# Shifts, scaled V and the normalising product on GpSimd in a gated attention and Mish kernel

## The chip, the cores and the metric

The kernel runs on one core of a Trainium2 chip. The metric is device time in microseconds. A core has TensorE (PE, matrix products), ScalarE (ACT, exponentials and tables), VectorE (DVE) and GpSimd (POOL); SyncE (SP) issues the DMAs here. TensorE writes only to PSUM, eight banks of 128 x 512 fp32; the others exchange tiles through SBUF.

## The reference

```python
g = sigmoid((x * gate_w).sum(-1, keepdims=True))       # x: 1 x 2048 x 640, bf16
qkv = (x @ wqkv), split into q, k, v of 32 heads of 20
a = softmax(q @ k.T * 20 ** -0.5) @ v, heads put together, @ wo
h = x @ w1 + b1                                        # 640 -> 1536
b = (h * tanh(softplus(h))) @ w2                       # Mish, 1536 -> 640
out = g * a + (1 - g) * b
```

## The kernel before

**Groups.** Attention runs over 32 groups: eight fours of heads (p) times four chunks of 512 queries (qc); the first five fours go chunk by chunk, the last three run inside each chunk. In a group, 16 blocks of 128 keys (j) times four heads make 64 score banks, 2048 in all. A visit of TensorE to the scores (L1118) multiplies row tiles of 32, up to four at once, one for each head. The products with V (L1211) are quads: four heads side by side in column tiles of 32, added up in one PSUM bank, acc, over the whole group. Dense work (q, k, v, Mish's two layers, the output product; all through product, L530) also uses column tiles. TensorE changes tiling between a visit to the scores and anything else.

**Two ways to an exponential.** ACT takes two or three score banks at once (L1168) and writes E. In their stead DVE can take a *set*, the four heads of one key block: four powers (power_of, L436) turn score banks into bf16 bit patterns through an int16 product, and two *shifts* (L494) add 43 and 86 to the patterns of the whole 128 x 2048 tile. The three tiles T are multiplied by V and by two scaled copies of V (VD, made by scale, L387), and their sum is the exponential's part. So a set takes four banks from ACT, costs DVE four powers and two shifts, and costs TensorE three V quads for one. VD is there for the last ND key blocks alone.

**The end of a group.** normalise (L1225) transposes acc from PSUM (L1232, a), takes reciprocals (L1246, b), multiplies by them (L1253, c) and stores four pieces of o to DRAM through SP. load_o (L871) brings o back transposed for the output product.

**The order.** Nothing is scheduled while the kernel runs. A planner in the kernel, the loop from L1614, steps through modelled time with fixed costs for each engine (an exponential of two banks 904 ns, a power or shift 600, a quad of 512 columns 216, a change of tiling 100) and writes out each engine's instructions in the order that it finds. Every engine then works strictly in that order and waits where a tile is not ready. `rule` holds the planner's choices, and PLAN changes them by progress in groups: LEAD is the number of sets that may be drawn for a group, KEEP3 and Q3 say when three banks may go to ACT at once, HEAT and HROOM when an idle TensorE multiplies by zeros (L1472). DVE's jobs wait in `dve_q`, with a priority and a time from which they are overdue.

**Buffers.** Seven of the eight PSUM banks are shared by scores and dense products; acc has its own. NHOLD tiles T hold sets, the other NTS - NHOLD (U_slots) hold shifted copies. NST staging tiles (st) carry q and k to DRAM, two tiles (ot) carry output rows, and two tiles (od) hold the transposed o.

Of the kernel before, what the change touches and what calls it, by code (L numbers as in the profile page):

```python
# [9 lines left out]
P = 128  # L10
# [48 lines left out]
INF = 1.0e18  # L59
# [3 lines left out]
def kernel(  # L63
# [35 lines left out]
    LOG2E = 1.4426950408889634  # L99
    ND = 6  # L100
    NLAST = 3
# [18 lines left out]
    NWARM = 6  # L120
    NTS = 9
    NHOLD = 5
    MOPEN = 3
# [12 lines left out]
    RING = 18  # L136
    NST = 2

# [26 lines left out]
    PLAN = {  # L165
        0.0: {'AHEAD': 5000.0, 'BEHIND': 6000.0, 'D2': 0.5, 'DQ': 1, 'DQ3': 2, 'DQ4': 2, 'ETIGHT': 0, 'HEAT': 0.9, 'HROOM': 0.0, 'KEEP3': 3, 'LEAD': 6, 'LOW': 0.5, 'MARGIN': 60.0, 'MERGE': 0, 'NEAR': 9, 'NOPEN': 3, 'PVMAX': 4, 'Q3': 2, 'ROOM': 200.0, 'SWTH': 520.0, 'VF': 0, 'VMIN': 2, 'WAIT1': 2000.0, 'WAIT2': 6000.0, 'WAITU': 100000.0},
        1.0: {'DQ3': 1, 'HROOM': 100.0, 'LOW': 0.6, 'MARGIN': 0.0, 'SWTH': 600.0, 'WAIT2': 100000.0},
        2.0: {'DQ': 2, 'MARGIN': 30.0},
        3.0: {'AHEAD': 1000.0, 'ETIGHT': 1, 'NEAR': 7, 'VF': 2, 'VMIN': 1, 'WAITU': 0.0},
        4.0: {'DQ': 3, 'LOW': 0.44, 'SWTH': 520.0, 'VF': 0},  # L170
        5.0: {'DQ4': 1, 'KEEP3': 2, 'LOW': 0.56, 'VMIN': 3, 'WAIT1': 0.0},
        6.0: {'LEAD': 5, 'MERGE': 1, 'Q3': 3},
        7.0: {'DQ': 2, 'NOPEN': 2},
        8.0: {'BEHIND': 4000.0, 'DQ4': 2, 'MERGE': 0},
        9.0: {'BEHIND': 2000.0, 'D2': 1.0},
        10.0: {'BEHIND': 6000.0},
        11.0: {'BEHIND': 4000.0, 'VMIN': 2, 'WAITU': 100000.0},
        12.0: {'BEHIND': 6000.0, 'MARGIN': 100.0},
        13.0: {'DQ4': 1, 'NOPEN': 4, 'PVMAX': 3},
        14.0: {'HEAT': 0.8, 'LOW': 0.41, 'MARGIN': 60.0, 'MERGE': 1, 'ROOM': 100.0},  # L180
        16.0: {'DQ': 1, 'DQ3': 3, 'NEAR': 12, 'ROOM': 300.0},
        17.0: {'MERGE': 0, 'SWTH': 250.0, 'VF': 2, 'WAIT2': 6000.0},
        18.0: {'PVMAX': 4, 'Q3': 1, 'WAIT1': 2000.0},
        19.0: {'BEHIND': 3000.0, 'ROOM': 100.0, 'VMIN': 1},
        20.0: {'LOW': 0.53, 'ROOM': 200.0},
        21.0: {'PVMAX': 2, 'SWTH': 300.0, 'WAIT2': 30000.0},
        22.0: {'LEAD': 6, 'MARGIN': 100.0, 'SWTH': 250.0},
        23.0: {'AHEAD': 5000.0, 'BEHIND': 2000.0, 'PVMAX': 4, 'SWTH': 450.0, 'WAIT1': -2000.0},
        24.0: {'DQ3': 0, 'DQ4': 0, 'LEAD': 5, 'MARGIN': 0.0, 'NEAR': 7, 'Q3': 2},
        25.0: {'BEHIND': 4000.0, 'DQ4': 3, 'KEEP3': 3, 'LOW': 0.41, 'WAITU': -200000.0},  # L190
        26.0: {'ETIGHT': 0, 'HROOM': 0.0, 'KEEP3': 2},
        27.0: {'HROOM': -200.0, 'NEAR': 9, 'ROOM': 100.0},
        29.0: {'AHEAD': 1000.0, 'PVMAX': 3, 'SWTH': 520.0, 'WAIT1': 2000.0, 'WAIT2': 100000.0},
        30.0: {'BEHIND': 6000.0},
        31.0: {'KEEP3': 0, 'VMIN': 2},
    }
# [289 lines left out]
    def d_shifts(d, t):  # L486
        G, j = d["G"], d["j"]
        pv_items[G].append((t, j, (0, d["T"], d["slot"])))

        def shift(i, t):  # L490
            slot = t_slot(U_slots, t)
            slot.users = 4
            tile_ = work.tile([P, 4 * QC], BF16, tag=slot.tag, name="T")
            nc.vector.tensor_scalar(  # L494
                out=tile_[:, :].bitcast(I16), in0=d["T"][:, :].bitcast(I16),
                scalar1=float(SHIFT[i]), scalar2=None, op0=ALU.add,
            )
            d["T%d" % i] = (tile_, slot)
            d["slot"].users -= 1
            d["slot"].free_at = max(d["slot"].free_at, t + 700.0)  # L500

        def can(t):
            return (
                pv_G[0] >= G and vd_ready.get(groups[G][0], INF) <= t
                and t_slot(U_slots, t) is not None
            )

        for i in range(1, NSH + 1):
            dve(
                t, t, 600.0, (lambda t, i=i: shift(i, t)), prio=2, can=can,  # L510
                done=lambda t, i=i: pv_items[G].append((t, j, (i,) + d["T%d" % i])),
            )

# [90 lines left out]
    def dense_chain(kind, i, c, start, due):  # L604
# [19 lines left out]
        def evac():  # L624
# [65 lines left out]
    def v_chain(sts, w, c0, n, start, due, gate=False):  # L690
# [18 lines left out]
        def evac():  # L709
# [174 lines left out]
    def load_b(s):  # L884
        if s not in bl and s < NS and bl_slots and b_left[s // NU] == 0:
# [3 lines left out]
            nc.sync.dma_start(out=bl[s][:, :], in_=b_dram[s * P : (s + 1) * P, :])  # L889

    def wo_chain(s, half, start, due):
        c, u = divmod(s, NU)
# [20 lines left out]
        def evac():  # L913
            ps = box["ps"]

            def copy(t):
# [308 lines left out]
    def normalise(G, ready):  # L1225
# [26 lines left out]
        def c(t):  # L1252
            nc.vector.tensor_tensor(  # L1253
                out=T2[i][:, :].rearrange("p (b r) -> p b r", r=32)[:, :, 0:DH],
# [23 lines left out]
        def c_done(t):  # L1278
# [4 lines left out]
            for k in range(4):  # L1283
# [6 lines left out]
                )  # L1290
            if p == NQ - 1:
                load_o(qc, D, t)
            elif p == NQ - NSB - 1 and qc == LQ:
                load_o(qc, (NQ - NSB) * HF, t)

# [127 lines left out]
    def step_pe(t):  # L1423
# [40 lines left out]
        def heat(room):  # L1464
# [6 lines left out]
            for t_ in range(4):  # L1471
                nc.tensor.matmul(  # L1472
                    acc[32 * t_ : 32 * t_ + DH + 1, :],
                    lhsT=zero_w[:, 0 : DH + 1], rhs=xT[:, 0, 0:QC], start=False, stop=False,
                    tile_position=(0, 32 * t_), skip_group_check=True,
# [236 lines left out]
```

## Time and profile before

| | us |
|---|---|
| median of 3 runs | 736.36 (731.82, 736.36, 736.46) |
| the profiled execution's own time | 730.75 |
| its span, first to last instruction | 729.0 |
| first and last exponential start | 10.9, 719.2 |
| first and last shift start | 47.4, 718.0 |
| ACT busy / DVE busy / GpSimd busy | 708.2 / 680.9 / 5.2 |

Busy times count overlapping instructions once, so busy time divided by the count is the pace of a group, while the mean of one is its length. Ends of matmuls are modelled, so TensorE is best read from the starts. TensorE's granted clock is 1.00 in each stretch of 100 us. Each row of the groups gives line, engine, operation, tiles written and read, shapes, count, busy time, mean ns of one, then idle time before it and what ended that.

### The profile page before, as it was taken

How to read it: one execution, taken by the hardware profiler on the slowest of the kernel's cores; microseconds unless marked ns; L12 is line 12 of the kernel's file. 1: busy time of each engine (PE TensorE's matmuls, PEld its weight loads, DVE VectorE, ACT ScalarE, POOL GpSimd, SP SyncE). 2: the span in 40 equal slices, each digit the busy share in tenths (PEclk: the TensorE clock that was granted, in tenths of full speed). 3: DMA queues.
4: the chain of work that ended last, by engine and by line, in shares of the span. 5: the costliest groups of instructions: out<-in, count | busy, mean ns of one | idle time of the engine just before them, and what ended most of it. 6: DMA issues, size and time to landing. Idle time of an engine off the chain costs nothing.

```text
span 729.0 us, 24381 instructions
## 1 busy us (share of the span) xinstructions
PE 714.5 (98%) x10390; PEld 233.5 (32%) x10390; DVE 680.9 (93%) x1214; ACT 708.2 (97%) x742; POOL 5.2 (1%) x12
## 2 busy tenths in 40 slices
PE   7999999999999999999999999999999999999987
PEld 4433332222222333333333222222333333333323
DVE  4499999999999989999999999899989999999987
ACT  6899999999999999999999999999999999999995
POOL 2000000000000000000000000000000000000000
PEclk9999999999999999999999999999999999999999
DMA  9511121131411211012130223311104210413421
GB/s 246 177 24 34 36 59 36 30 81 40 86 32 40 49 45 24 12 15 41 43 92 26 44 41 87 81 54 25 30 22 74 56 38 25 65 43 61 75 75 55
DMA packets 125612, 40.46 MB, mean 56 GB/s; under 512 B 91136, under 2 KB 124944, under 8 KB 125504
## 3 DMA queue, kind: packets, MB, share of 16 engines
q1 hardware_dynamic: 123904, 38.38, 24.1%
q8 instruction: 81, 1.33, 0.8%
q10 hardware_dynamic: 1600, 0.53, 0.3%
q14 instruction: 27, 0.22, 0.1%
HBM read 23.61 MB, written 12.79 MB: 50 GB/s over the span
## 4 chain that ended last, share of the span: by engine, by line
PE 72%; ACT 16%; issue 5%; DVE 4%; DMA 2%; SPq 1%; DVEq 0%
PE Sp L1118 25%; PE Sp L530 24%; PE Sp L1211 22%; ACT E L1168 16%; DVE T L436 2%; DVE T L494 1%; DMA w_top<-in_A_wqkv_dram 1%; PE Sp L1472 1%; DMA kT<-k_dram 1%; DVE st L632 0%; DMA out_dram<-ot 0%; DVE ot L925 0%; PE Sp L1653 0%; PE Sp L1329 0%; DMA q_dram<-st 0%
## 5 line engine op out<-in xcount | busy, mean ns | idle before, releaser
L1168 ACT ACTIVATE E<-Sp 128x1024 bf16<-128x1024 f32 (+1 forms) x726 | 677.0, 1114 | 6.4 <-PE Sp L1118 5.9
L436 DVE TENSOR_SCALAR T<-Sp 128x512 int16<-128x512 f32 (+1 forms) x572 | 375.6, 685 | 14.5 <-PE Sp L1118 13.6
L1118 PE MATMUL Sp<-qT,kT 32*128 32x512 bf16 x2048 | 290.9, 384 | 5.3 <-ACT E L1168 1.9
L494 DVE TENSOR_SCALAR T<-T 128x2048 int16<-128x2048 int16 x288 | 192.2, 680 | 0.7
L1118 PEld LDWEIGHTS <-kT 32*128 32x128 bf16 x2048 | 76.4, 91 | 272.9 <-issue 269.2
L1211 PE MATMUL Sp<-E,VA 128*21 128x512 bf16 x1472 | 140.4, 382 | 0.0
L1211 PE MATMUL Sp<-T,VD 128*21 128x512 bf16 x1152 | 106.1, 382 | 0.0
L530 PE MATMUL Sp<-w_sb,big 128*32 128x320 bf16 x1536 | 77.8, 301 | 0.0
L530 PE MATMUL Sp<-xT,w1t 128*32 128x512 bf16 x960 | 76.1, 384 | 0.2 <-DVE T L436 0.2
L1211 PEld LDWEIGHTS <-VA 128*21 128x21 bf16 x2048 | 44.0, 90 | 64.2 <-issue 55.7
L1211 PE MATMUL Sp<-T,VA 128*21 128x512 bf16 x576 | 54.5, 382 | 0.0
L530 PE MATMUL Sp<-xT,ws 128*32 128x512 bf16 x720 | 53.9, 383 | 0.0
L530 PEld LDWEIGHTS <-big 128*32 128x32 bf16 x1536 | 33.7, 95 | 27.7 <-issue 20.0
L1211 PEld LDWEIGHTS <-VD 128*21 128x21 bf16 x1152 | 26.9, 90 | 30.7 <-issue 25.7
L778 DVE TENSOR_SCALAR big<-Sp,b1f 128x512 bf16<-128x512 f32 x48 | 35.6, 742 | 1.1 <-PE Sp L530 0.8
L530 PE MATMUL Sp<-wo_sb,od 128*32 128x320 bf16 (+1 forms) x608 | 32.7, 302 | 2.0 <-DVE ot L925 2.0
L530 PE MATMUL Sp<-wv,xT 128*32 128x81 bf16 (+2 forms) x960 | 33.9, 258 | 0.2 <-DVE st L632 0.2
L632 DVE CAST st<-Sp 128x512 bf16<-128x512 f32 x36 | 24.6, 683 | 5.0 <-PE Sp L530 3.5
L530 PEld LDWEIGHTS <-w1t 128*32 128x32 bf16 x960 | 18.1, 94 | 27.7 <-issue 24.6
L1232 DVE STREAM_TRANSPOSE T<-Sp 128x512 f32<-128x512 f32 x32 | 22.7, 708 | 0.9 <-PE Sp L1211 0.6
L713 DVE CAST VA<-Sp 128x80 bf16<-128x80 f32 (+2 forms) x48 | 16.2, 373 | 7.1 <-PE Sp L530 7.1
L530 PEld LDWEIGHTS <-xT 128*32 128x32 bf16 x960 | 18.0, 96 | 14.6 <-issue 12.3
(72 smaller groups left out, 196.0 us busy)
## 6 DMA issues: line engine op xcount, KB each, us to landing
w1t<-in_B_w_dram SPq DMA_DIRECT2D x24, 320.0 KB
q_dram<-st SPq DMA_DIRECT2D x20, 128.0 KB
b_dram<-bt SPq DMA_DIRECT2D x16, 160.0 KB
bl<-b_dram SPq DMA_DIRECT2D x16, 160.0 KB
out_dram<-ot SPq DMA_DIRECT2D x16, 160.0 KB
qT<-q_dram SPq DMA_DIRECT2D x124, 20.0 KB
o_dram<-T SPq DMA_DIRECT2D x120, 20.0 KB
kT<-k_dram SPq DMA_DIRECT2D x28, 80.0 KB
```

The costliest lines, as they stand in the source:

```text
L436: nc.vector.tensor_scalar(out=dst.bitcast(I16), in0=src, scalar1=inv_sqrt_dh * LOG2E * 128.0, scalar2=127.0 * 128.0 + BETA, op0=ALU.mult, ...
L494: nc.vector.tensor_scalar(out=tile_[:, :].bitcast(I16), in0=d["T"][:, :].bitcast(I16), scalar1=float(SHIFT[i]), scalar2=None, op0=ALU.add,)
L530: nc.tensor.matmul(out_[k : k + 32], lhsT=lhsT[:, k : k + 32], rhs=rhs, tile_position=(0, k), **kw)
L632: nc.vector.tensor_copy(out=res["st"][:, :], in_=ps[:, :])
L713: nc.vector.tensor_copy(out=VA[:, sts[i], h0 : h0 + nh, 0:DH], in_=ps[:, i, 0:n].rearrange("p (h d) -> p h d", d=DH),)
L778: nc.vector.tensor_scalar(out=big[:, slot.tag, (ft % 2) * QC : (ft % 2 + 1) * QC], in0=ps[:, :], scalar1=b1f[:, ft : ft + 1], scalar2=None ...
L1118: nc.tensor.matmul(ps_cols, lhsT=kT[p][32 * t_ : 32 * t_ + 32, j * P : (j + 1) * P], rhs=qT[G][32 * t_ : 32 * t_ + 32, :], tile_position=( ...
L1168: nc.scalar.activation(E[:, x : x + n, :], ps, ACT.Exp, scale=inv_sqrt_dh,)
L1211: nc.tensor.matmul(acc[32 * t_ : 32 * t_ + DH + 1, :], lhsT=lhsT, rhs=rhs, start=(pv_done[G] == 0), stop=(pv_done[G] == pv_total[G] - 1), ...
L1232: nc.vector.transpose(out=st["T1"][:, :, :].rearrange("p b r -> p (b r)"), in_=acc[:, :])
L1472: nc.tensor.matmul(acc[32 * t_ : 32 * t_ + DH + 1, :], lhsT=zero_w[:, 0 : DH + 1], rhs=xT[:, 0, 0:QC], start=False, stop=False, tile_posit ...
```

## The change

It moves three kinds of work from VectorE to GpSimd: the shifts (but for the last group, NDV = 1), the scaled copies of V, and the product with the reciprocals (but for the last group). The planner gets a fourth engine with a queue `pool_q`, worked by (group, time), with costs of its own: 1840 ns for a shift and 140 until others see it, 620 for a product. A shift may now also start one group ahead if at least UEARLY = 2 tiles are free.

Buffers: ND 8 for 6, NTS 11 for 9, NHOLD 6 for 5 (so five U tiles for four), three st and three ot tiles, each with a time from which the planner holds it free. The transposed o lies in the columns of xT of its chunk and is fetched in two parts. The dummy products read w2_sb in place of xT. PLAN is another table throughout.

```diff
-    ND = 6
+    ND = 8
-    NTS = 9
-    NHOLD = 5
+    NTS = 11
+    NHOLD = 6
-    NST = 2
+    NST = 3
+    PCOST = 1840.0
+    PTAIL = 140.0
+    UEARLY = 2
+    NDV = 1
+    NOT = 3
     PLAN = {
-        0.0: {..., 'KEEP3': 3, 'LEAD': 6, 'Q3': 2, ...},
-        5.0: {..., 'KEEP3': 2, ...},
-        6.0: {'LEAD': 5, 'MERGE': 1, 'Q3': 3},
-        18.0: {..., 'Q3': 1, ...},
-        22.0: {'LEAD': 6, ...},
-        24.0: {..., 'LEAD': 5, 'Q3': 2},
-        25.0: {..., 'KEEP3': 3, ...},
-        26.0: {..., 'KEEP3': 2},
-        31.0: {'KEEP3': 0, 'VMIN': 2},
+        0.0: {..., 'KEEP3': 3, 'LEAD': 6, 'Q3': 2, ...},
+        2.0: {..., 'KEEP3': 2, 'Q3': 1, ...},
+        3.0: {'KEEP3': 1, ...},
+        4.0: {..., 'Q3': 2},
+        5.0: {..., 'KEEP3': 3},
+        6.0: {'KEEP3': 1, 'Q3': 1, ...},
+        7.0: {..., 'LEAD': 5, ...},
+        8.0: {'KEEP3': 3, 'LEAD': 7},
+        9.0: {..., 'Q3': 3, ...},
+        10.0: {..., 'Q3': 1, ...},
+        12.0: {..., 'KEEP3': 2, 'LEAD': 8, ...},
+        17.0: {..., 'LEAD': 5, ...},
+        21.0: {'LEAD': 7, 'Q3': 2, ...},
+        22.0: {'LEAD': 6, ...},
+        27.0: {..., 'LEAD': 5, ...},
+        29.0: {'Q3': 1, ...},
+        31.0: {..., 'LEAD': 3, ...},
     }
@@ make_vd
-            nc.vector.tensor_scalar(
+            nc.gpsimd.tensor_scalar(
                 out=VD[p][:, :, i, :],
...
-            dve(t, t, 200.0, (lambda t, i=i: scale(i, t)), prio=1, done=done)
+            pool_q.append((
+                (-1, t), 70.0 + 0.86 * ND * 4 * (DH + 1), lambda t: True,
+                (lambda t, i=i: scale(i, t)), done,
+            ))
@@ d_shifts
-            nc.vector.tensor_scalar(
+            eng = nc.vector if G >= NG - NDV else nc.gpsimd
+            eng.tensor_scalar(
                 out=tile_[:, :].bitcast(I16), in0=d["T"][:, :].bitcast(I16),
                 scalar1=float(SHIFT[i]), scalar2=None, op0=ALU.add,
             )
...
+            pool_q.append((
+                (G, t), PCOST, can, (lambda t, i=i: shift(i, t)),
+                (lambda t, i=i: pv_items[G].append((t, j, (i,) + d["T%d" % i]))),
+            ))
@@ load_o
-        od[qc] = work.tile([P, KT, QC], BF16, tag=f"od{qc % 2}", name="od")
+        if qc not in od:
+            od[qc] = xT[:, :, qc * QC : (qc + 1) * QC]
@@ normalise
-            dve(t, t, 140.0, b, prio=pr, done=lambda t: dve(t, t, 420.0, c, prio=pr, done=c_done))
+            dve(t, t, 140.0, b, prio=pr, done=lambda t: pool_q.append(
+                ((G - 0.5, t), 620.0, lambda t: True, c, c_done)
+            ))
...
-            nc.vector.tensor_tensor(
+            nc.gpsimd.tensor_tensor(
                 out=T2[i][:, :].rearrange("p (b r) -> p b r", r=32)[:, :, 0:DH],
...
+    def step_pool(t):
+        for it in sorted(pool_q, key=lambda it: it[0]):
+            if it[0][1] <= t and it[2](t):
+                pool_q.remove(it)
+                it[3](t)
+                it[4](t + it[1] + PTAIL)
+                return it[1]
+        return None
```

More of the change, by code (lines that the diff above doesn't have):

```diff
@@ L136 @@
     RING = 18
-    NST = 2
+    NST = 3
[3 more added lines that the diff above has]
+    NDV = 1
+    TRD = -0.2
+    FKD = -0.1
+    NOT = 3
     rule = Rule()
@@ L165 @@
     PLAN = {
[L166 to L169, printed above, removed]
@@ L170 @@
-        4.0: {'DQ': 3, 'LOW': 0.44, 'SWTH': 520.0, 'VF': 0},
-        5.0: {'DQ4': 1, 'KEEP3': 2, 'LOW': 0.56, 'VMIN': 3, 'WAIT1': 0.0},
-        6.0: {'LEAD': 5, 'MERGE': 1, 'Q3': 3},
[L173 to L194, printed above, removed]
@@ L195 @@
-        31.0: {'KEEP3': 0, 'VMIN': 2},
+        0.0: {'AHEAD': 2000.0, 'BEHIND': 6000.0, 'D2': 0.5, 'DQ': 3, 'DQ3': 2, 'DQ4': 2, 'ETIGHT': 1, 'HEAT': 0.7, 'HROOM': 0.0, 'KEEP3': 3, 'LEAD': 6, 'LOW': 0.5, 'MARGIN': 60.0, 'MERGE': 0, 'NEAR': 99, 'NOPEN': 5, 'PVMAX': 4, 'Q3': 2, 'ROOM': 200.0, 'SWTH': 250.0, 'VF': 0, 'VMIN': 1, 'WAIT1': 0.0, 'WAIT2': 6000.0, 'WAITU': -200000.0},
+        1.0: {'HEAT': 0.8, 'ROOM': 100.0},
+        2.0: {'DQ3': 1, 'KEEP3': 2, 'Q3': 1, 'ROOM': 200.0, 'VF': 2},
+        3.0: {'KEEP3': 1, 'MARGIN': 0.0, 'ROOM': 100.0},
@@ new lines @@
+        4.0: {'DQ4': 1, 'HROOM': -200.0, 'PVMAX': 2, 'Q3': 2},
+        5.0: {'AHEAD': 3000.0, 'KEEP3': 3},
+        6.0: {'KEEP3': 1, 'NOPEN': 4, 'Q3': 1, 'VF': 0},
+        7.0: {'D2': 1.0, 'DQ4': 3, 'LEAD': 5, 'LOW': 0.38, 'NOPEN': 5},
+        8.0: {'KEEP3': 3, 'LEAD': 7},
+        9.0: {'PVMAX': 4, 'Q3': 3, 'WAITU': 0.0},
+        10.0: {'DQ': 1, 'Q3': 1, 'VF': 2, 'WAIT2': 3000.0},
+        11.0: {'NOPEN': 3},
+        12.0: {'HEAT': 0.9, 'KEEP3': 2, 'LEAD': 8, 'NEAR': 12, 'NOPEN': 4, 'SWTH': 300.0, 'VF': 0},
@@ new lines @@
+        13.0: {'ETIGHT': 0, 'HEAT': 0.7, 'PVMAX': 3, 'VF': 2, 'WAITU': -200000.0},
+        15.0: {'HROOM': 0.0},
+        16.0: {'PVMAX': 4, 'WAITU': 0.0},
+        17.0: {'DQ4': 1, 'LEAD': 5, 'NEAR': 7, 'NOPEN': 5, 'WAITU': 100000.0},
+        18.0: {'HROOM': -200.0, 'PVMAX': 3},
+        19.0: {'NEAR': 99},
+        20.0: {'PVMAX': 2},
+        21.0: {'LEAD': 7, 'LOW': 0.53, 'PVMAX': 3, 'Q3': 2},
+        22.0: {'LEAD': 6, 'LOW': 0.6, 'NEAR': 7, 'ROOM': 200.0, 'WAIT1': -2000.0, 'WAITU': 0.0},
@@ L196 @@
+        23.0: {'HEAT': 0.8, 'MERGE': 1, 'NEAR': 5},
+        24.0: {'HEAT': 0.9, 'PVMAX': 4},
+        25.0: {'DQ4': 3, 'HROOM': 0.0, 'MERGE': 0, 'NEAR': 9, 'ROOM': 100.0},
+        27.0: {'AHEAD': 5000.0, 'LEAD': 5, 'PVMAX': 3, 'WAIT1': 0.0},
+        28.0: {'DQ': 2, 'MARGIN': 30.0, 'NOPEN': 4, 'VF': 1},
+        29.0: {'Q3': 1, 'VF': 0},
+        31.0: {'AHEAD': 2000.0, 'HROOM': 100.0, 'LEAD': 3, 'MARGIN': 0.0},
+        32.0: {'LOW': 0.56, 'VMIN': 3},
     }
@@ L354 @@
     dve_q = []
+    pool_q = []
     act_q = deque()
     seq = [0]
-    free = {"PE": 0.0, "ACT": 0.0, "DVE": 0.0}
+    free = {"PE": 0.0, "ACT": 0.0, "DVE": 0.0, "POOL": 0.0}
     mode = [None]
@@ L360 @@
     s_left = [64] * NG
-    idle = {"PE": 0.0, "ACT": 0.0, "DVE": 0.0}
+    idle = {"PE": 0.0, "ACT": 0.0, "DVE": 0.0, "POOL": 0.0}
     def dve(t, ready, cost, fn, prio=1, done=None, can=None, born=INF):
@@ L499, in shift @@
             d["slot"].users -= 1
-            d["slot"].free_at = max(d["slot"].free_at, t + 700.0)
+            d["slot"].free_at = max(d["slot"].free_at, t + PCOST + 100.0)
         def can(t):
[L503 to L506, printed above, removed]
+            if vd_ready.get(groups[G][0], INF) > t:
+                return False
+            n = sum(1 for s_ in U_slots if s_.users == 0 and s_.free_at <= t)
+            return n > 0 and (pv_G[0] >= G or (pv_G[0] == G - 1 and n >= UEARLY))
         for i in range(1, NSH + 1):
[L509 to L512, printed above, removed]
+            if G >= NG - NDV:
+                dve(
+                    t, t, 600.0, (lambda t, i=i: shift(i, t)), prio=2, can=can,
+                    done=lambda t, i=i: pv_items[G].append((t, j, (i,) + d["T%d" % i])),
+                )
+                continue
+            pool_q.append((
+                (G, t), PCOST, can, (lambda t, i=i: shift(i, t)),
+                (lambda t, i=i: pv_items[G].append((t, j, (i,) + d["T%d" % i]))),
+            ))
     def mm_pieces(n, fn, each):
@@ L639, in done @@
                 stored[(kind, i, c)] = t + 2500.0
+                slot.free_at = t + 2800.0
             return [(600.0, copy)], done
@@ L644, in dense_chain @@
             start, due, mm_pieces(KT, piece, MM), evac,
-            lambda t: x_ok(c, t) and (kind, i) in strips and t >= (5000.0, 10000.0)[min(i, 1)],
+            lambda t: x_ok(c, t) and (kind, i) in strips and t >= (5000.0, 10000.0)[min(i, 1)]
+            and stages[0].free_at <= t + 500.0,
         )
@@ L734, in v_chain @@
         return Chain(
-            start, due, mm_pieces(KT * len(sts), piece, max(65.0, width / 2.4)), evac,
+            start, due, mm_pieces(KT * len(sts), piece, max(36.0, width / 2.4)), evac,
             lambda t: t >= (0.0 if gate else W_ARRIVE) and all(x_ready.get(st, INF) <= t for st in sts),
@@ L869, with load_o @@
     LQ = NQC - 1
-    def load_o(qc, upto, t):
-        od[qc] = work.tile([P, KT, QC], BF16, tag=f"od{qc % 2}", name="od")
-        for k in range(-(-upto // P)):
+    def load_o(qc, blocks):
+        if qc not in od:
+            od[qc] = xT[:, :, qc * QC : (qc + 1) * QC]
+        for k in blocks:
             nc.sync.dma_start(
@@ L878, in load_o @@
             )
-        o_ready[qc] = t + 8000.0
     bl_slots = ["bl0", "bl1", "wkp"]
@@ L889, in load_b @@
             nc.sync.dma_start(out=bl[s][:, :], in_=b_dram[s * P : (s + 1) * P, :])
+    ot_free = {}
+    begun = set()
     def wo_chain(s, half, start, due):
@@ L900, in piece @@
                 box["ps"] = bank_tile([P, HALF])
+                begun.add(s)
                 load_b(s)
@@ L922, in copy @@
                     if half == 0:
-                        ots[s] = work.tile([P, D], BF16, tag=f"ot{s % 2}", name="ot")
+                        ots[s] = work.tile([P, D], BF16, tag=f"ot{s % NOT}", name="ot")
                     o = ots[s][:, cols]
@@ L934, in done @@
                     nc.sync.dma_start(out=out2d[s * P : (s + 1) * P, :], in_=ots[s][:, :])
+                    ot_free[s % NOT] = t + 6000.0
             return [(430.0, copy)], done
@@ L941, in wo_chain @@
                 s in bl or (len(bl_slots) > 0 and b_left[c] == 0)
-            ),
+            ) and (s in begun if half else tail or ot_free.get(s % NOT, 0.0) <= t),
         )
@@ L950 @@
         for u in range(NU):
-            chains.append(transpose_chain(NU * c + u, -1.0, 0.25 * c - 0.2 + 0.01 * u))
-        chains.append(first_k_chain(c, -1.0, 0.25 * c - 0.1))
+            chains.append(transpose_chain(NU * c + u, -1.0, 0.25 * c + TRD + 0.01 * u))
+        chains.append(first_k_chain(c, -1.0, 0.25 * c + FKD))
     for a in range(0, NS, 4):
@@ L1290, in c_done @@
                 )
[L1291 to L1294, printed above, removed]
+            last_p = NQ - 1 - (NSB if qc == LQ else 0)
+            early = last_p * HF // P
+            if p == last_p - 1 and qc != LQ:
+                load_o(qc, range(early))
+            elif p == last_p:
+                load_o(qc, range(early, -(-(p + 1) * HF // P)))
+                o_ready[qc] = t + 9000.0
+                if qc == LQ - 1:
+                    load_o(LQ, range((NQ - NSB - 1) * HF // P))
         dve(0.0, ready, 640.0, a, prio=0, done=a_done)
@@ L1473, in heat @@
                     acc[32 * t_ : 32 * t_ + DH + 1, :],
-                    lhsT=zero_w[:, 0 : DH + 1], rhs=xT[:, 0, 0:QC], start=False, stop=False,
+                    lhsT=zero_w[:, 0 : DH + 1], rhs=w2_sb[:, 0, 0:QC], start=False, stop=False,
                     tile_position=(0, 32 * t_), skip_group_check=True,
@@ L1607, in step_dve @@
         return cost
-    steps = {"PE": step_pe, "ACT": step_act, "DVE": step_dve}
+    def step_pool(t):
[6 more added lines that the diff above has]
+        return None
+    steps = {"PE": step_pe, "ACT": step_act, "DVE": step_dve, "POOL": step_pool}
     t = 0.0
@@ L1613 @@
     plan = sorted(PLAN)
-    while pv_G[0] < NG or chains or chain[0] or dve_q or act_q:
+    while pv_G[0] < NG or chains or chain[0] or dve_q or act_q or pool_q:
         while plan and prog[0] >= plan[0]:
@@ L1627 @@
                 ev[1](t)
-        for eng in ("DVE", "ACT", "PE"):
+        for eng in ("POOL", "DVE", "ACT", "PE"):
             if free[eng] <= t:
```

## The prediction

> **What bounds the kernel now.** I read the engine totals first, then the groups kept apart by shape, then single starts in a busy stretch.
>
> ```profile
> PE 714.5 (98%) x10390; PEld 233.5 (32%) x10390; DVE 680.9 (93%) x1214; ACT 708.2 (97%) x742; POOL 5.2 (1%) x12
> ```
>
> ```profile
> L1168 ACT ACTIVATE E<-Sp 128x1024 bf16<-128x1024 f32 x704 | 651.2, 1103 | 6.4 <-PE Sp L1118 5.9 <-ACT E L1168 0.2
> L436 DVE TENSOR_SCALAR T<-Sp 128x512 int16<-128x512 f32 x568 | 370.8, 681 | 14.5 <-PE Sp L1118 13.6
> L1118 PE MATMUL Sp<-qT,kT 32*128 32x512 bf16 x2048 | 290.9, 384 | 5.3 <-ACT E L1168 1.9 <-ACT qT L1338 1.0 <-DVE st L632 0.7
> L494 DVE TENSOR_SCALAR T<-T 128x2048 int16<-128x2048 int16 x288 | 192.2, 680 | 0.7
> ...
> L1168 ACT ACTIVATE E<-Sp 128x1536 bf16<-128x1536 f32 x21 | 31.4, 1495 | 0.0
> ...
> L1472 PE MATMUL Sp<-xT,zero_w 128*21 128x512 bf16 x176 | 15.6, 383 | 0.0
> ...
> L1253 DVE TENSOR_TENSOR T<-T,rec 128x320 bf16<-128x320 f32 x31 | 14.9, 481 | 0.2
> ```
>
> Three engines are full at once and GpSimd is empty. Busy divided by count is the pace, since neighbours overlap: an exponential of two banks costs ACT 651.2/704 = 0.925 us, a power costs DVE (370.8 + 4.8 of four merged ones)/576 = 0.652, a shift 0.667. The 288 shifts are two for each of 144 sets; each set is four powers. So DVE takes 576 of the 2048 score banks, ACT 704 x 2 + 21 x 3 + 1 = 1472.
>
> A PE busy share is modelled, so I look at starts in TensorE's timeline:
>
> ```profile
> 306.79 0.39 PE L1118 MATMUL Sp<-qT,kT 32*128 32x512 bf16 x3
> 307.12 0.40 PE L1211 MATMUL Sp<-T,VD 128*21 128x512 bf16 x4
> 307.34 0.39 PE L1211 MATMUL Sp<-E,VA 128*21 128x512 bf16 x4
> 307.66 0.39 PE L1118 MATMUL Sp<-qT,kT 32*128 32x512 bf16 x3
> ```
>
> A V quad costs 307.34 - 307.12 = 0.22. The loop of one visit to the scores and two quads takes 0.87, so a visit costs 0.87 - 0.44 = 0.43, whether it makes two, three or four banks: about half of it is the change to the other tiling and back. Nearly every start from 100 to 700 us keeps this spacing, so TensorE is really full, and so is ACT (starts 0.903 apart at the median). The waits count the visits, and show how little waits for DMA:
>
> ```profile
> PEld L1118 <- issue: 269.2, 722, 1.0
> ...
> DVE ot L925 <- DMA out_dram<-ot: 2.1, 1, 2.1
> ...
> DVE st L632 <- DMA q_dram<-st: 1.4, 1, 1.4
> ```
>
> TensorE's sum: 722 visits x 0.43 = 310; V quads (1472 + 1152 + 576)/4 = 800 x 0.22 = 176; 44 dummy quads (L1472, 176/4) x 0.22 = 10. The other 233 of 729 are dense products, start and end, which the change leaves as they are.
>
> **What moves, and the size of it.** The planner may draw sets up to LEAD for a group. Weighting LEAD by the groups in which it holds gives 168 before, of which 144 were drawn (0.857), and 195 after. With the same share: 167 sets, 23 more.
>
> ACT: 92 banks fewer x 0.925/2 = -42.5 us, so ACT alone would allow 729 - 42.5 = 686.5.
>
> DVE: 668 powers x 0.652 = 436, and the other work, 680.9 - 375.6 - 192.2 - 14.9 (products L1253) - 3.9 (scaled V) = 94, plus some 6 shifts of the last group, 4: 534 us. It stops being near a bound (76% of 706).
>
> TensorE: 46 more V quads x 0.22 = +10.1. ACT's 92 banks are 46 visits fewer x 0.43 = -19.8. Three-bank exponentials save half a visit each. Nine of the 21 in the trace lie at 430 to 475 us, in the stretch with Q3 = 1 (groups 18 to 23); the new rules hold Q3 at 1 for about 19 groups and a less loaded DVE gives banks back sooner. At 9 for six groups, 13 more groups are 20 more; KEEP3 = 1 in four groups takes me to 40, between 0 and 80: -20 visits, -8.6. Half the dummy quads go, between none and all (0 to -9.7): -4.8. Sum -23.1: 705.9, with ends 729 + 10.1 - 19.8 = 719.3 and 729 + 10.1 - 19.8 - 17.2 - 9.7 = 692.4.
>
> GpSimd shows no shift before. The nearest rows are its fills and its select:
>
> ```profile
> L328 POOL MEMSET VA<- 128x512 bf16 x1 | 2.4, 2367 | 0.0
> ...
> L1343 POOL MEMSET wo<- 128x640 bf16 x2 | 1.2, 631 | 5.0 <-PE Sp L1329 5.0
> masks.py:199 POOL TENSOR_SCALAR_AFFINE_SELECT ident<-ident 128x128 bf16<-128x128 bf16 x1 | 0.3, 292 | 0.1
> masks.py:197 POOL MEMSET ident<- 128x128 bf16 x1 | 0.2, 204 | 0.0
> L314 POOL MEMSET zero_w<- 128x32 bf16 x1 | 0.1, 124 | 0.3 <-POOLq L1696 0.3
> ```
>
> The dense fills lie on a line: (631 - 124)/608 = 0.834 ns an element, 97 ns fixed. For 2048 elements that is 1.81 us. A shift also reads; the select reads and takes 88 ns more than a fill of its size. If that is fixed, a shift takes 1.89; if it is per element (0.69 ns), 3.21. The strided fill of VA at 2367/512 = 4.6 ns an element (9.5 us) is far, as shifts are dense. DVE's 0.68 is the end below. I take 1.85, between the first two, since DVE's rows show reading beside writing: its fill of 128x1024 takes 0.91 us and its shift, which also reads, 0.68 for 4 KB a partition alike. The planner reckons with PCOST = 1.84, so its order fits if that is right. The product (320 elements, two inputs) lies between 0.36 and 0.81; 0.62 taken, near the middle. The scaled V (672 elements): 0.66 to 1.12; 0.70 taken. GpSimd's sum: 334 - 6 = 328 shifts x 1.85 = 607, 31 x 0.62 = 19, 16 x 0.70 = 11: 637 us. It can start where the first shift starts now, 47 us, and must end about 10 us before the last row: 694. That is inside 706, with 12 us of room.
>
> What the moves queue: TensorE's order is fixed at build time, so a V quad of a shifted tile that GpSimd has not finished holds every later matmul, and with it ACT. Until now DVE gave the tile after 0.67 us, now it comes 1.2 us later; UEARLY lets shifts start one group ahead and there are five U tiles for four, so I cost this at nothing; uncovered at each of 31 group changes it is 31 x 1.2 = 37 us. The products on GpSimd can stand behind one shift (1.85), and four stores of o each stand in SP's queue behind them, with later q and k loads behind those. These are needed a group (some 21 us) later: nothing, else 1.85 x 31 = 57. The third st and ot tiles end waits of 1.4 and 2.1 us on DVE, which is no longer the bound: 0 taken of -3.5 to 0. The transposed loads of o into xT are as many as before (19), most a group earlier; xT of a chunk is last read by dense products well before: 0, at worst one wait like the 3.89 us that a kT load shows in the chain.
>
> The Trainium skill speaks against such a move: GPSIMD Engine Reference, section "Elementwise — side-by-side cycle accounting", puts its best ordinary loop at 1.8 cycles an element, which as an estimate would be 3.07 us a shift, though the same section lets a body of one or two operations run at 1.03 cycles, 1.76 us. By the first the sum would be some 1100 us, by the second the forecast stands.
>
> **Rivals.** (1) GpSimd becomes the bound, the case on the slow side. Its price is 57 us of start and end, 30 of products and scaled V, and 328 x p for the shifts, so it decides from p = (729 - 87)/328 = 1.96 us, only 6% over what I take. At 2.1 the span is 776; at 3.21, reading paid per element, 1140. For it: the narrow margin and that no row shows GpSimd at such a form. Against: dense fills of four sizes (1, 32, 128 and 640) lie on the one line. Chance 0.2. The skill's 1.8 cycles is this rival.
>
> (2) DVE and GpSimd block each other in SBUF. The one strided fill beside DVE fills took 2367; the next dense fill took 686 where the line gives 524. Fully serial, 534 + 637 + 57 = 1228; blocked one time in five of DVE's 534, GpSimd ends at 694 + 107 = 801. Against: DVE's 0.68 us for 2048 elements leaves the middle of the kernel, and what stays there takes that long for 512 and reads PSUM. Chance 0.06. The Trainium skill (SBUF — State Buffer, "Who interferes with whom") lets such one-input reads run beside GpSimd; no run here shows it yet.
>
> (3) The freed DVE buys nothing since TensorE binds: sets stay near 144, or each visit saved is spent on V quads and fills. Then 719 to 735. For it: TensorE is already full. Chance 0.14, and this is also the case that the change does not do what it says.
>
> (4) Forecast: chance 0.6.
>
> **How the numbers follow.** Span 705.9; the profiled execution takes 1.75 us more than its span (730.75 against 729.0): 707.7. The median of the runs is 736.36/730.75 = 1.0077 of the profiled one: 713. Its own ends: 692.4 and 719.3 give 699 and 727. About 1% (729 to 744) is what this measurement can tell from no change. Rivals 1 and 2 lie above 744, up to 1.2 ms; rival 3 gives 726 to 742, a quarter of it still under 729. So faster 0.63 (0.6 + 0.14/4), same 0.11, slower 0.26. The range runs from 692 (more three-bank exponentials) to 770 (GpSimd at 2.06 us); outside are most of rivals 1 and 2, 0.18, and little below.
>
> **What would show it.** GpSimd rows of 128x2048 at 1.85 us a start, GpSimd busy near 95% from 47 us on; about 334 shifts, 668 powers and 1380 banks on ACT; 650 to 665 issue waits before scores; DVE under 80%. Wrong: shifts over 1.96 us; TensorE's V quads waiting for GpSimd; DVE powers longer than 0.65; or still 288 shifts with TensorE full.

## The result and the profile after

The changed kernel takes 1744.65 us (median; 1741.63 to 1744.87) against 736.31: a ratio of 2.374, 95% interval 2.366 to 2.383. The forecast was 713, with a range of 692 to 770. Its span is 1743.1 us. The page's engine totals, and the groups by shape (line, engine, operation, tiles, shapes, count, then busy time, mean ns of one, and idle time before it):

```profile
PE 1037.6 (60%) x10378; PEld 272.7 (16%) x10378; DVE 562.3 (32%) x917; ACT 747.4 (43%) x712; POOL 1635.0 (94%) x355
...
PEclk9666666676766665666766666656756666655668
```

```profile
L506 POOL TENSOR_SCALAR T<-T 128x2048 int16<-128x2048 int16 x296 | 1579.2, 5364 | 33.7 <-DVE T L447 23.2 <-PE Sp L1144 7.4 <-DVE rec L1274 2.2
L1194 ACT ACTIVATE E<-Sp 128x1024 bf16<-128x1024 f32 x642 | 641.3, 1026 | 905.0 <-PE Sp L1144 901.4 <-PE Sp L1237 1.6
L447 DVE TENSOR_SCALAR T<-Sp 128x512 int16<-128x512 f32 x604 | 410.9, 688 | 1040.1 <-PE Sp L1144 1032.1 <-POOL T L506 5.2 <-ACT E L1194 0.8
...
L1237 PE MATMUL Sp<-T,VD 128*21 128x512 bf16 x1208 | 162.0, 524 | 693.5 <-POOL T L506 693.1
...
L395 POOL TENSOR_SCALAR VD<-VA 128x672 bf16<-128x672 bf16 x16 | 30.3, 1891 | 34.4 <-DVE z_t L742 33.4
...
L1281 POOL TENSOR_TENSOR T<-T,rec 128x320 bf16<-128x320 f32 x31 | 22.6, 728 | 4.6 <-DVE rec L1276 4.6
```

One row is the whole result: a shift holds GpSimd for 1579.2/296 = 5.33 us, and GpSimd works for 94% of the span. Everything else waits in a line behind it. TensorE's V quads of shifted tiles stand still for 693 us for L506; ACT and DVE in their turn wait for TensorE's scores, 901 and 1032 us. The timeline shows one such wait:

```profile
810.83 5.37 POOL L506 TENSOR_SCALAR T<-T 128x2048 int16<-128x2048 int16 x1
816.25 0.61 PE L1237 MATMUL Sp<-T,VD 128*21 128x512 bf16 x4 [7.05 <-POOL T L506]
...
816.91 0.72 DVE L1258 STREAM_TRANSPOSE T<-Sp 128x512 f32<-128x512 f32 x1 [6.88 <-PE Sp L1237]
```

A quad that could not start held TensorE for 7.05 us, and DVE for the end of the group with it. The same matmul now lasts 0.61 us instead of 0.40: TensorE's granted clock is 0.66 on average. The clock is low because TensorE stands still, not the other way round: with shorter shifts, below, it is 0.994 in the same order.

### The profile page after: what moved, and what is told of

Its sections match the earlier page's. It is cut to its first block, busy times and chain, and to the rows that moved or that the text cites. A ratio compares the mean times of both kernels' runs of the same rounds, so it can differ in the third digit from the quotient of the medians.

```text
span 1743.1 us, 24646 instructions
## 1 busy us (share of the span) xinstructions
PE 1037.6 (60%) x10378; PEld 272.7 (16%) x10378; DVE 562.3 (32%) x917; ACT 747.4 (43%) x712; POOL 1635.0 (94%) x355
## 5 line engine op out<-in xcount | busy, mean ns | idle before, releaser
L506 POOL TENSOR_SCALAR T<-T 128x2048 int16<-128x2048 int16 x296 | 1579.2, 5364 | 33.7 <-DVE T L447 23.2
L1194 ACT ACTIVATE E<-Sp 128x1024 bf16<-128x1024 f32 (+1 forms) x696 | 716.2, 1058 | 980.1 <-PE Sp L1144 976.2
L447 DVE TENSOR_SCALAR T<-Sp 128x512 int16<-128x512 f32 x604 | 410.9, 688 | 1040.1 <-PE Sp L1144 1032.1
L1237 PE MATMUL Sp<-T,VD 128*21 128x512 bf16 x1208 | 162.0, 524 | 693.5 <-POOL T L506 693.1
L1144 PE MATMUL Sp<-qT,kT 32*128 32x512 bf16 x2048 | 374.9, 513 | 3.8 <-DMA qT<-q_dram 2.1
L1237 PE MATMUL Sp<-E,VA 128*21 128x512 bf16 x1444 | 185.8, 520 | 0.0
L548 PE MATMUL Sp<-w_sb,big 128*32 128x320 bf16 x1536 | 114.3, 403 | 0.0
L548 PE MATMUL Sp<-xT,w1t 128*32 128x512 bf16 x960 | 109.3, 527 | 0.0
L395 POOL TENSOR_SCALAR VD<-VA 128x672 bf16<-128x672 bf16 x16 | 30.3, 1891 | 34.4 <-DVE z_t L742 33.4
L548 PEld LDWEIGHTS <-xT 128*32 128x32 bf16 (+1 forms) x1568 | 38.9, 114 | 42.2 <-issue 33.5
L548 PE MATMUL Sp<-wo_sb,xT 128*32 128x320 bf16 (+1 forms) x608 | 41.6, 386 | 0.6 <-DVE big L950 0.6
```

The lines of the kernel that those rows point to most:

```text
L395: nc.gpsimd.tensor_scalar(out=VD[p][:, :, i, :], in0=VA[:, NS - ND : NS, 4 * p : 4 * p + 4, :].rearrange("p j h d -> p j (h d)"), scalar1= ...
L447: nc.vector.tensor_scalar(out=dst.bitcast(I16), in0=src, scalar1=inv_sqrt_dh * LOG2E * 128.0, scalar2=127.0 * 128.0 + BETA, op0=ALU.mult, ...
L506: eng.tensor_scalar(out=tile_[:, :].bitcast(I16), in0=d["T"][:, :].bitcast(I16), scalar1=float(SHIFT[i]), scalar2=None, op0=ALU.add,)
L548: nc.tensor.matmul(out_[k : k + 32], lhsT=lhsT[:, k : k + 32], rhs=rhs, tile_position=(0, k), **kw)
L1144: nc.tensor.matmul(ps_cols, lhsT=kT[p][32 * t_ : 32 * t_ + 32, j * P : (j + 1) * P], rhs=qT[G][32 * t_ : 32 * t_ + 32, :], tile_position=( ...
L1194: nc.scalar.activation(E[:, x : x + n, :], ps, ACT.Exp, scale=inv_sqrt_dh,)
```

## The experiments

**What a shift costs on GpSimd by itself.** A kernel of its own runs GpSimd's forms alone, then beside DVE:

```diff
+    for k in range(4):
+        g.tensor_scalar(out=dA[k % 2][:, :], in0=src[:, :], scalar1=43.0, scalar2=None, op0=ALU.add)
...
+    for k in range(4):
+        g.tensor_scalar(
+            out=dA[k % 2][:, :].bitcast(BF16), in0=src[:, :].bitcast(BF16),
+            scalar1=0.5, scalar2=1.0, op0=ALU.mult, op1=ALU.add,
+        )
...
```

> A kernel of its own that computes nothing of the reference: GpSimd instructions of ten forms alone, four of each (int16 add of a scalar at 2048, 1024 and 512 elements, bf16 multiply with one and with two operations, fp32 multiply of 1024, bf16 copy, bf16 add of two tensors, int32 add of two tensors at 1024, the same with a broadcast operand); then DVE's powers and shifts alone; then GpSimd's shift beside DVE's powers, and beside DVE's shifts. Theory A (the shift is slow by itself on GpSimd, some 0.16 us and 2.5 ns an element, by the two shapes 128x672 and 128x2048 of the changed kernel): 5.3 us alone at 2048, 2.7 at 1024, 1.4 at 512, and the same beside powers. Rival B (DVE holds GpSimd up): 1.8 to 1.9 us alone at 2048, over 5 only beside DVE. The int32 add of two tensors at 1024 elements should take 1.9 us by the product's row (0.69 for 320).

Groups by shape. L67 is the shift alone, L69 and L71 the same at half and quarter length, L73 a bf16 multiply, L78 a multiply and an add, L85 a copy, L91 and L95 the int32 add without and with a broadcast operand, L110 the shift beside DVE's powers, L118 and L120 GpSimd's and DVE's shifts side by side:

```profile
L120 DVE TENSOR_SCALAR dD<-src 128x2048 int16<-128x2048 int16 x24 | 31.7, 1397 | 0.0
L118 POOL TENSOR_SCALAR dA<-src 128x2048 int16<-128x2048 int16 x4 | 22.5, 5644 | 0.1
...
L110 POOL TENSOR_SCALAR dA<-dD 128x2048 int16<-128x2048 int16 x4 | 21.7, 5436 | 10.9 <-DVE dD L107 10.9
L67 POOL TENSOR_SCALAR dA<-src 128x2048 int16<-128x2048 int16 x4 | 21.4, 5364 | 4.7 <-DVE src L47 4.7
L73 POOL TENSOR_SCALAR dA<-src 128x2048 bf16<-128x2048 bf16 x4 | 21.4, 5363 | 0.1
...
L69 POOL TENSOR_SCALAR dA<-src 128x1024 int16<-128x1024 int16 x4 | 11.0, 2767 | 0.0
L91 POOL TENSOR_TENSOR dA<-src,cst 128x1024 int32<-128x1024 int32 x4 | 9.2, 2337 | 0.0
L78 POOL TENSOR_SCALAR dA<-src 128x2048 bf16<-128x2048 bf16 x4 | 7.5, 1897 | 0.0
L95 POOL TENSOR_TENSOR dA<-src,cst 128x1024 int32<-128x1024 int32 x4 | 7.4, 1890 | 0.0
L85 POOL COPY dA<-src 128x2048 bf16<-128x2048 bf16 x4 | 7.4, 1891 | 0.0
L71 POOL TENSOR_SCALAR dA<-src 128x512 int16<-128x512 int16 x4 | 5.8, 1487 | 0.0
```

Alone the shift takes the same 5.36 us as in the kernel. So theory A stands and rival B, contention with DVE, falls: beside powers the four take 21.7 us instead of 21.4, and the 0.3 lies in the first of them, which began while DVE's last shift still ran. (The powers in this test start 0.725 us apart instead of 0.598, but here they all write one tile; in the second kernel of this kind, below, they keep the 0.725 after GpSimd has stopped.) The price is 2.5 ns an element ((5.35 - 2.75)/1024). The surprise is L78: the same instruction with a second operation, and a first of multiply, takes a third, 7.5/4 = 1.87, as long as a copy.

**Is the shift's price the whole cause?** The shift is cut to a length that costs what the planner reckons with:

```diff
+    PW = 664
...
+            w = 4 * QC if G >= NG - NDV else PW
             eng.tensor_scalar(
-                out=tile_[:, :].bitcast(I16), in0=d["T"][:, :].bitcast(I16),
+                out=tile_[:, 0:w].bitcast(I16), in0=d["T"][:, 0:w].bitcast(I16),
...
-                rhs = tile_[:, t_ * QC : (t_ + 1) * QC]
+                rhs = tile_[:, 0:QC] if i and G < NG - NDV else tile_[:, t_ * QC : (t_ + 1) * QC]
```

> The changed kernel, but GpSimd's shifts write only the first 664 of 2048 columns, and the products with VD read the first 512 columns for all four heads; the last group is whole. By A's line a shift then takes 0.16 + 664 x 2.53 = 1.84 us, which the planner reckons with. Theory A: TensorE's clock is back at 1.0 and the span falls to what TensorE's own sum gives for the 151 sets drawn: 694 visits x 0.43 + 814 quads x 0.22 + 27 dummy quads x 0.22 + 233 = 716, so 705 to 730. Rival C (not the price of the shift but the order, the buffers or the new rules cost the time): well over 760.

Measured in one run: 732.93 us (kernel before 731.05 on the same chip), span 731.1, shifts 1.834 us apart, clock 0.994. So 1012 of the 1014 us over the kernel before go with the shift's price, and the low clock with them. The span lies 1 us over the expected range; where the 15 us over 716 come from is taken up below.

**The shifts back on VectorE, in the order made for GpSimd.**

```diff
-            eng = nc.vector if G >= NG - NDV else nc.gpsimd
+            eng = nc.vector
```

> The changed kernel with the shifts back on VectorE, in the order in which the planner issues them for GpSimd; the scaled V and the product stay on GpSimd. Theory A: DVE is busy 562 + 296 x 0.61 = 743 us and becomes the bound, clock 1.0: 750 to 800. Rival C: over 1000, as the order stays.

Measured in one run: 769.25 us, span 767.5, clock 0.998. The span is in A's range, so the order alone is no disaster. DVE is busy for 697.5 us (91%), not for 743. That DVE holds TensorE up is seen at the starts: of 36 that come over 0.6 us after the one before, 21 follow a wait for a power of DVE.

**The shift as an int32 add.** One word holds two patterns, so half as many elements do:

```diff
+    two = consts.tile([P, 4], I16, tag="two")
+    for i in (1, 2):
+        nc.gpsimd.memset(two[:, 2 * i - 2 : 2 * i], SHIFT[i])
...
-            eng.tensor_scalar(
-                out=tile_[:, :].bitcast(I16), in0=d["T"][:, :].bitcast(I16),
-                scalar1=float(SHIFT[i]), scalar2=None, op0=ALU.add,
-            )
...
+                nc.gpsimd.tensor_tensor(
+                    out=tile_[:, :].bitcast(I32), in0=d["T"][:, :].bitcast(I32),
+                    in1=two[:, 2 * i - 2 : 2 * i].bitcast(I32).to_broadcast([P, 2 * QC]), op=ALU.add,
+                )
```

> The changed kernel with GpSimd's shift as an int32 add of two tensors over 1024 words (each word two bf16 patterns, the second operand one word 43 or 86 in both halves, broadcast). Nothing else changed. By the product's row (0.69 us for 320 elements, 0.16 fixed) 1.9 us a shift. Theory A: the span falls to 715 to 760. If two inputs cost much more at that length, say 2.5 us: 48 + 296 x 2.5 + 53 + 40 = 880.

Measured in one run: 745.43 us, span 743.6, shifts 1.850 us apart. The price is as expected, the span in the upper half of the range: 12.5 us more than with 664 columns, for 0.016 us more a shift (296 x 0.016 = 4.7). The pages show where the 12.5 lie: TensorE stands idle for 4.0 us more (743.6 - 716.6 against 731.1 - 708.1), and the same 10378 matmuls keep it busy for 8.5 us more. In five stretches of 3.4 or 6.8 us, 23.9 us in all, the granted clock is 0.50; with 664 columns there are two, 6.8 us. One of the five (stretch, busy time of PE, PEld, DVE, ACT and POOL, granted clock, DMA share, GB/s):

```profile
448.50:455.10 6.60, 6.43 (x49) 1.20 (x51) 3.51 (x6) 3.49 (x5) 4.83 (x4) 0.50 0.01 2
```

17.1 us more at half speed are 8.5 us. Each of the five begins within 2 us of the end of an idle time of TensorE of 0.8 to 2.1 us; that such waits bring the half clock on is read from this, and not tested.

**Which second operation makes it fast?**

```diff
+    for k in range(4):
+        g.tensor_scalar(
+            out=dA[k % 2][:, 0:2048], in0=src[:, 0:2048], scalar1=1.0, scalar2=43.0, op0=ALU.mult, op1=ALU.add,
+        )
...
+    for k in range(4):
+        g.tensor_scalar(
+            out=dA[k % 2][:, 0:2048], in0=src[:, 0:2048], scalar1=43.0, scalar2=0.0, op0=ALU.add, op1=ALU.add,
+        )
```

> A kernel of its own that computes nothing of the reference: GpSimd's tensor_scalar with different pairs of operations, four of each: int16 times 1 plus 43 at 2048, 1024 and 664 elements; plus 43 plus 0; plus 43 times 1; bf16 times 0.5 times 1; bf16 times 0.5 plus 0 at 672; int16 plus 43 alone at 672; a copy of 664. m1 showed one operation at 5.34 us for 2048 and multiply-then-add at 1.86. Theory A1 (only multiply-then-add has a fast path): 1.86, 0.98 and 0.67 us for the first three, 0.65 to 0.7 for 672 of bf16, and 5.34 for the other pairs at 2048. Rival A2 (any second operation makes it fast): 1.86 for all pairs at 2048. Alone at 672: 1.85 in both.

Groups by shape. L67, L71, L75: int16 times 1 plus 43 at 2048, 1024, 664; L79: plus 43 plus 0; L83: plus 43 times 1; L87: bf16 times 0.5 times 1; L91: bf16 times 0.5 plus 0 at 672; L95: int16 plus 43 alone at 672:

```profile
L79 POOL TENSOR_SCALAR dA<-src 128x2048 int16<-128x2048 int16 x4 | 28.3, 7092 | 0.1
L67 POOL TENSOR_SCALAR dA<-src 128x2048 int16<-128x2048 int16 x4 | 7.6, 1900 | 4.9 <-DVE src L47 4.7
L83 POOL TENSOR_SCALAR dA<-src 128x2048 int16<-128x2048 int16 x4 | 7.6, 1900 | 0.3
L87 POOL TENSOR_SCALAR dA<-src 128x2048 bf16<-128x2048 bf16 x4 | 7.5, 1902 | 0.1
L95 POOL TENSOR_SCALAR dA<-src 128x672 int16<-128x672 int16 x4 | 7.5, 1893 | 0.1
...
L91 POOL TENSOR_SCALAR dA<-src 128x672 bf16<-128x672 bf16 x4 | 2.9, 758 | 0.0
```

Neither A1 nor A2 as written: each pair with a multiply is fast, in either order, but plus and plus is slower than one plus (7.1 us). The int16 pairs leave a gap of 0.08 us behind each (idle 0.3 against 0.1 for the group), so they start 1.98 apart where bf16 starts 1.86 apart.

**The shift with two operations, and then the scaled V too.**

```diff
-                scalar1=float(SHIFT[i]), scalar2=None, op0=ALU.add,
+                scalar1=1.0, scalar2=float(SHIFT[i]), op0=ALU.mult, op1=ALU.add,
...
-                scalar1=RATIO[i + 1], scalar2=None, op0=ALU.mult,
+                scalar1=RATIO[i + 1], scalar2=0.0, op0=ALU.mult, op1=ALU.add,
```

The first hunk alone:

> The changed kernel with the shift on GpSimd written as times 1, plus 43 or 86: the same values, two operations. Nothing else changed. Theory A: a shift takes 1.86 us as in m1, the price that the planner reckons with, and the span is that of the run with 664 columns, 731 (725 to 740), clock over 0.98. Rival: if the low price needs bf16, the shift stays at 5.3 and the span at 1743.

Measured: 772.65 us, 1.055 times the kernel before (1.051 to 1.059), span 770.7. The shifts are 1.980 us apart, 0.12 more than expected from bf16, and 40 us more in all than with 664 columns.

Both hunks:

> As before, and the scaled V is also written with two operations (times the ratio, plus 0). In the run with 664 columns TensorE stood still for 23.3 us in gaps over 0.6 us against 8.3 in the kernel before; the longest lie where the four of heads changes, and the planner holds a scaled V at 648 ns where it takes 1854. Theory D (the rest is the scaled V's price): 0.65 us for one, the gaps fall by some 12 us and the span to 716 (708 to 722), 1 to 3% under the kernel before. Rival E (GpSimd's late handing over in general): 725 to 735.

Measured: 753.17 us, ratio 1.029 (1.025 to 1.032), span 754.0. Both D and E missed, as both took the shift at 1.86. The step itself is near what D says, 731 to 716: 770.7 - 754.0 = 16.7 us off the span, for 16 scaled V of 1.1 us less each. Of these, 9.2 us are idle time of TensorE and 7.5 are its busy time. In two other pairs of runs (664 columns and int32, without this hunk and with it) the same edit is worth 10.9 and 20.9 us. TensorE's waits for GpSimd's shifts (us in total, times, longest), first hunk alone and then both:

```profile
PE Sp L1237 <- POOL T L506: 34.1, 49, 2.7
```

```profile
PE Sp L1237 <- POOL T L506: 23.2, 46, 1.4
```

**Buffers and rules without GpSimd.**

```diff
-    NDV = 1
+    NDV = 32
...
-            pool_q.append((
-                (-1, t), 70.0 + 0.86 * ND * 4 * (DH + 1), lambda t: True,
-                (lambda t, i=i: scale(i, t)), done,
-            ))
+            dve(t, t, 200.0, (lambda t, i=i: scale(i, t)), prio=1, done=done)
...
```

> The changed kernel's buffers and PLAN, with all three kinds of work on VectorE again and the planner told so (NDV = 32, scaled V and product as before the change). Tells what buffers and rules do without GpSimd. Theory A: DVE carries the shifts again, some 93% busy, so nothing is won: 728 to 760. Rival F (buffers and rules are what is worth something): under 722.

Measured in one run: 743.0 us against 731.75, span 741.2, DVE busy 92%. By themselves, buffers and this PLAN win nothing.

**Planned prices everywhere.** The 664 columns and the whole int32 shift, each as above with one hunk more:

```diff
-                scalar1=RATIO[i + 1], scalar2=None, op0=ALU.mult,
+                scalar1=RATIO[i + 1], scalar2=0.0, op0=ALU.mult, op1=ALU.add,
```

> The run with shifts of 664 columns (1.834 us from start to start, as the planner reckons), and the scaled V with two operations. The two runs with whole two-operation shifts stood at 770.7 and 754.0 without and with the cheap scaled V: 16.7 us. Theory A (each us that GpSimd is later than planned is a us of the whole, since TensorE's order is fixed and its queue has no slack): 731.1 - 16.7 = 714.4, beside the forecast's sum for 151 sets, 716: 710 to 720, so 1.5 to 2.5% faster than the kernel before. Rival G (the remaining time is TensorE's and ACT's own): 725 to 733.

Measured: 722.22 us, ratio 0.980 (0.973 to 0.988), span 720.2: just over the range of A, and well under that of G. TensorE waits 0.4 us for GpSimd's shifts, 10.4 before this hunk.

> The int32 shift (whole, the reference's values; 1.85 us from start to start, 743.6 us of span) with the two-operation scaled V. Theory A: 743.6 - 16.7 = 727 (722 to 732), level with the kernel before or just under it. Rival G: 738 to 745.

Measured: 724.55 us, ratio 0.984 (0.977 to 0.990), span 722.7, in A's range. This is the changed kernel's whole work, and faster than the kernel before, by 1.6% here and 1.2% in the repetition below. The page's totals, GpSimd's shift and scaled V, and the two waits that were 976 and 693 us in the changed kernel:

```profile
PE 707.6 (98%) x10378; PEld 234.7 (32%) x10378; DVE 546.5 (76%) x917; ACT 696.3 (96%) x712; POOL 588.0 (81%) x357
```

```profile
L515 POOL TENSOR_TENSOR T<-T,two 128x1024 int32<-128x1024 int32 x296 | 550.5, 1895 | 59.3 <-DVE T L451 41.2 <-PE Sp L1246 9.2 <-PE Sp L1153 8.8
...
L399 POOL TENSOR_SCALAR VD<-VA 128x672 bf16<-128x672 bf16 x16 | 12.1, 753 | 32.9 <-DVE z_t L751 31.8
```

```profile
ACT E L1203 <- PE Sp L1153: 10.3, 13, 2.3
...
PE Sp L1246 <- POOL T L515: 1.3, 4, 0.5
```

TensorE waits 1.3 us for GpSimd in all, and is full again.

**PLAN picked again for the measured prices,** beside the last kernel on one chip:

```diff
-    PCOST = 1840.0
+    PCOST = 1860.0
...
-                ((G - 0.5, t), 620.0, lambda t: True, c, c_done)
+                ((G - 0.5, t), 720.0, lambda t: True, c, c_done)
...
```

> The int32 shift and the two-operation scaled V, with the planner told what the runs measured (1860 ns for a shift, 720 for a product, 820 for a scaled V, 222 for a V quad, 104 for a change of tiling) and PLAN picked again for these costs; 144 sets are drawn instead of 151. Theory H (wrong costs in the planner still lose time): 708 to 718. Rival I (TensorE, busy 98% and still for 11 us in the last run, is the bound, and another order saves no visits): 718 to 728, level with the last run.

Measured: 742.86 us, ratio 1.0135 (1.0109 to 1.0160), span 741.3: both theories miss. 18 of TensorE's starts come over 0.6 us after the one before, 21.8 us in all (12 and 11.4 in the last run), all at scores and dense products, none at a V quad: it is no longer GpSimd that TensorE waits for. The longest, 4.0 us, follows a wait of DVE for a load from DRAM (bl), by which DVE gave its banks back late:

```profile
552.75 1.47 DVE L962 SCALAR_TENSOR_TENSOR ot<-Sp,g_t,bl 128x320 bf16<-128x320 f32 x3 [4.95 <-DMA bl<-b_dram]
```

What makes this order the worse one as a whole stays open.

> The last run again, unchanged, on the same chip as the new order, for the comparison: 720 to 728.

Measured: 723.34 us, ratio 0.9875 (0.9853 to 0.9897), span 723.7. It repeats: a gain, and a small one.

## Why the prediction was wrong

**The step that failed is GpSimd's price of a shift.** The prediction put 1.85 us, from a line through four dense fills, between readings of 1.81 and 1.89, with 3.21 as the worst. It measured 5.33. A fill says what GpSimd writes in a given time and nothing of what computing takes; the one computing row, the select, was 88 ns over a fill at 128 elements, and even its worst reading fell short by two fifths. The argument that settled it, that DVE reads beside writing at no cost, was taken from another engine. PCOST = 1.84 seemed to support it; it is near the pace of a multiply and an add in bf16 (1.86), not that of the one add that the code issues.

**Rival 1 was what happened,** at a chance of 0.2 and at a price over both that it named (2.1 and 3.21). Its formula gives 57 + 30 + 296 x 5.33 = 1665 for the shifts that were really queued; the span is 1743. Its lower bound of 1.96 us for the turn was wrong too. It reckoned that GpSimd has room until its sum fills the span. At 1.98 us (scaled V cheap) the formula gives 673, and 754 was measured with GpSimd busy 80%. What counts is not the sum but how late each tile comes against the plan: from 664 columns to the whole two-operation shift a start takes 0.146 us longer, 296 x 0.146 = 43 us, and the span grew by 39.6 (scaled V dear) and 33.8 (cheap), 0.8 to 0.9 us for each us. The prediction has no term for this. The delay that it did cost, at nothing ("What the moves queue"), is another: a shift takes 1.2 us longer than on DVE, but the planner knows it. That was right: at the planned price TensorE waits 1.3 us for GpSimd in all. On a straight line between 1.85 (722.7) and 1.98 (754.0) the kernel before lies at about 1.88.

**In cycles.** The Trainium skill (GPSIMD Engine Reference, "Elementwise — side-by-side cycle accounting") named 1.8 and 1.03 cycles an element. At its 1.2 GHz, 2.54 ns is 3.0 cycles: the measured single operation is slower than either, and only the pair with a multiply or the copy (1.87/2048, 1.1 cycles) comes near the lower one.

**Rival 2 falls as the cause.** Powers and shifts do not hurt each other: 5.34 us alone, 5.34 beside, and powers that follow each other at once start 0.608 us apart in the kernel with GpSimd's shifts, 0.601 before. Shift beside shift they do (last section).

**What held, and what did not.** TensorE's sum held in its form, not in its counts. There were 151 sets instead of 167, since 0.774 of LEAD was used and not 0.857; 53 three-bank exponentials instead of 61; 694 visits instead of 656; 814 V quads instead of 846; 27 dummy quads instead of 22. With these counts the sum is 694 x 0.43 + 814 x 0.22 + 27 x 0.22 + 233 = 716, and at the planned prices the span is 720 and 723. So a shift of 1.85 would not have given the forecast's 705.9 either: 722.7 lies in the band of rival 3 (719 to 735, TensorE binds), and the gain is 1.2 to 1.6% where 713 against 736.36 is 3.2%. It is small because TensorE was as full as DVE.

**Luck.** DVE's 534 us and 76% look right beside the 546.5 and 76% at the planned prices, but two errors cancel there. There are 604 powers and not 668, so the sum's own terms give 604 x 0.652 + 94 + 4 = 492. And the 94 of other work is what is left when the busy times of groups are taken from DVE's total; neighbours overlap, so this takes off too much. Counted by itself, with overlaps once, all that is no power, shift, product or scaled V is 158 us before and 162 after.

**The scaled V** was priced 0.70 and took 1.89, for the same reason as the shift: one operation. With two, its 30.3 us of GpSimd are 12.1, and the span falls by 10.9, 16.7 or 20.9 in the three pairs. In each, TensorE's idle time falls by 9 to 12 us; the rest, 2 to 9 us, is its busy time. The product, 0.62, took 0.69 to 0.73.

## What to carry to other kernels

Before work is moved to an engine that the trace shows idle, run the very instruction, with its operations and types, by itself: 5.34, 1.98 and 7.1 us are one int16 shape and one opcode, with an add, a multiply and an add, and two adds. In an order fixed at build time an engine need not be full to set the time; a producer 0.13 us a shift slower than planned cost 31 us at 80% busy. And the worth of freeing an engine is read from the others: with TensorE at 98% on both sides, a fifth of DVE's work (680.9 to 546.5 us) bought 1.2 to 1.6%. Busy times of groups that overlap cannot be taken from a total one by one.

## What the runs showed of the hardware

On GpSimd the single-operation tensor_scalar is the slow one: 2.5 ns an element in int16 and bf16, also in fp32 (1024 elements in 2.8 us), while a pair with a multiply takes 0.91 in bf16 and 0.97 in int16, and a bf16 copy 0.9. An int32 add with a broadcast operand takes 1.85 us for 1024 elements, with a full one 2.3.

DVE's shift and GpSimd's shift block each other whole. Three of DVE's beside GpSimd's lasted 5.84 us each instead of 0.70, started one for each of GpSimd's, and GpSimd's starts went from 5.34 to up to 5.76 apart; a DVE copy of two elements lasted 3.6 us. In the changed kernel the last group's shifts on DVE show it once: 3372 ns at most, 680 at the median; that one began 2.5 us into GpSimd's last shift and ended 0.6 us after it. This agrees with the Trainium skill (SBUF — State Buffer, "Who interferes with whom"): where DVE runs in a mode of two ports, the shared pair of ports is held for a whole instruction. That DVE's shift runs in such a mode is not shown here.

TensorE's granted clock fell to 0.66 when it was busy for 60% of the span in short bursts, and was 0.994 in the same program with shorter shifts. These are means: the traces of the kernels record 1.0 and 0.5 alone. But for the last one, at the end of a run, each stretch at 0.5 lasts 3.41 us or a multiple of it, up to 81.9, and in the changed kernel they make 1174 of the 1743 us.
